# Linear attention and two MLP layers: the squared layer's scale moved into the norm's weights, its sign and offset into later steps, a padded last chunk, and all pair sums made on chip

## Chip, cores and metric

One core of a Trainium2 chip runs the whole program. The metric is device time in microseconds (us) of one execution; it was measured three times, and one more execution was profiled. Engines are named as in the profile: PE (TensorE) with PEld for its weight loads, DVE (VectorE), ACT (ScalarE), POOL (GpSimd), SP (SyncE, which issues the transfers). PSUM is the memory that PE writes, in banks of 128 x 512.

## The reference, cut to what matters

```
kv  = einsum('bhsd,bhse->bhde', k, v)          # 8 batches, 8 heads, 576 positions, 64 wide
o   = einsum('bhsd,bhde->bhse', q, kv)
x   = o / sqrt(mean(o*o, -1) + 1e-6) * g_norm  # then 4608 tokens x 512
h   = x @ w_in1;  r = maximum(h, 0)
x   = (s * (r*r) + b) @ w_out1                 # 2048 hidden columns; s and b are single numbers
h   = x @ w_in2
out = (h * sigmoid(h)) @ w_out2
```

## The kernel before

All is fp32. A wide product is made of three passes (`mm3`): each operand is split into a rounded part, made by ACT (`rnd`), and the rest, made by DVE or POOL (`rest`), and high x high, high x low and low x high are summed in one PSUM bank.

Tokens come in nine blocks of 512. Attention runs for a pair of heads of one batch at a time (`attention_pair`): `kv` sums k'v over four chunks of 128 positions and a last one of the remaining 64, for two heads that stand in two halves of the columns; `normalize` squares, sums, takes the root and multiplies by the weights `gn`. The first layer treats blocks 0 to 4 as they come (`unit`: one block and 128 hidden columns, 80 units). In a unit PE makes h in 12 passes, ACT applies three steps to it in its bank (`first`, `squares`, `affine`) and rounds it (`g_hi`), DVE makes the rest (`g_lo`), and PE takes 12 more passes into four accumulator banks.

Blocks 5 to 8 of the first layer, and blocks 0 to 3 and 5 to 8 of the second, are taken two at a time as six pairs (`tp` 0 to 5, of which 0 and 1 are of the first layer). A pair replaces each 2 x 2 block product by seven products of sums (Strassen-Winograd). Sums of inputs come from `pair_direct` (loads of the blocks, four sums each for two column parts, rounding by ACT, rest by POOL), except in the last two pairs: their sums are formed by POOL out of the results of pairs 0 and 1 (`results`, line 1153), stored in `xt_d`, and loaded by `pair_x`. `hidden` makes the seven products into three banks and forms the hidden values; for the first layer each gets relu, square and the affine step (L1023, L1026, L1029) before DVE forms the further sums (`add_up`, L1005). `outputs` sums seven results over four quarters: the first is copied out of its accumulator bank (`copy`, L223 or L225), the others are added by DVE (L1109). `results` combines them on POOL (L1134). The last block of the second layer runs as plain units at the end.

Meanwhile the weights are decoded, split and summed in quarters of 128 x 256 (`rq`; L405 sums, L216 rounding, L219 rests) and kept in DRAM for the pairs.

What order stands on each engine is decided when the program is built: `Plan` takes every step with an engine and a cost in us, a key, and what it needs and gives, and lists them by when they could begin. So a change of a cost or a step shifts the order on all engines. Costs are the plan's own, such as

```
add({"PE": 0.97}, key, kv, needs=..., makes=[f("kv")], takes=[b["psk"]], gives=...)
add({ACT: 0.68}, u + 0.25, affine, needs=[("sq", u)], makes=[("aff", u)])
```

Names in rows: `kv_ps`, `o_ps`, `r_ps`, `m_ps` are banks of the attention, `h` and `hp` hold hidden values of units and pairs, `acc` accumulators, `tmp` temporaries of a pair, `ya` a pair's results, `gh` and `g` split hidden values, `xo` split inputs, `vecs` single columns for norm weights, s and b.

## Time and profile before

| | |
|---|---|
| three runs, us | 1588.6, 1588.15, 1590.71; median 1588.6 |
| the profiled execution, us | 1589.08, its span 1587.3 |
| mean granted PE clock | 0.997 of 2.4 GHz |
| busy, us | PE 1558.8 (98%), DVE 1075.8 (68%), ACT 914.3 (58%), POOL 641.6 (40%) |
| transfers | 366.49 MB, mean 231 GB/s |

The span runs from the first to the last instruction; the execution's time holds some 1.8 us around it. Passes of PE overlap, so a record's length (0.39 us for a wide one) is more than the distance from one start to the next. A row of grouped instructions names line, engine, operation, output and inputs, shape and count, then busy time, the mean of one in ns, and the idle time before them with what ended it. Lines are those of the kernel before unless the change is spoken of.

### The profile page before, as it was taken

The page shows a single profiled execution, that of the slowest core. Times are in us where ns is not written, and L with a number is a line of the kernel's source. Part 1 is how long each engine was busy: PE and PEld are TensorE (multiplying, and loading weights), DVE is VectorE, ACT ScalarE, POOL GpSimd, SP SyncE. Part 2 cuts the span into 40 slices and gives each one's busy share as a digit, 9 for nine tenths or more (in the row PEclk, how much of TensorE's full clock was granted, in tenths as well). Part 3 has the DMA queues.
Part 4 walks back from the last instruction along what each step waited for, and adds up shares of the span by engine and source line. Part 5 has one row for each costly group of instructions (what it writes and reads, how often), then busy time and mean ns, then how long its engine had stood idle before and what let it go on. Part 6 is the DMA issues. An engine that isn't in the chain of part 4 may idle for free.

```text
span 1587.3 us, 23243 instructions
## 1 busy us (share of the span) xinstructions
PE 1558.8 (98%) x7393; PEld 1263.9 (80%) x7393; DVE 1075.8 (68%) x1937; ACT 914.3 (58%) x1779; POOL 641.6 (40%) x585
## 2 busy tenths in 40 slices
PE   8999999999999999999899999999999999999999
PEld 6777888778878878887787888888888888888887
DVE  5787678877666568888788856765666566656521
ACT  5897667667677677676667443544354444444222
POOL 1331122122124234478637862762277237622410
PEclk9999999999999999999999999999999999999999
DMA  9665688987557768888988896878687767776684
GB/s 212 186 190 137 227 256 274 277 242 234 186 173 235 260 208 277 266 272 280 294 267 281 289 310 189 255 200 238 197 281 193 237 200 242 188 240 196 205 201 141
DMA packets 354395, 366.49 MB, mean 231 GB/s; under 512 B 175712, under 2 KB 237152, under 8 KB 354272
## 3 DMA queue, kind: packets, MB, share of 16 engines
q1 hardware_dynamic: 354144, 365.00, 76.1%
q8 instruction: 59, 0.97, 0.3%
q14 instruction: 64, 0.52, 0.1%
q0 software_dynamic: 128, 0.00, 0.0%
HBM read 274.73 MB, written 90.18 MB: 230 GB/s over the span
## 4 chain that ended last, share of the span: by engine, by line
PE 49%; DVE 2%; ACT 1%; POOL 1%; DMA 1%; issue 1%; ACTq 0%; POOLq 0%; DVEq 0%
PE hp L966 21%; PE acc L1100 8%; PE acc L1102 7%; PE acc L1101 7%; PE acc L775 1%; PE acc L773 1%; PE acc L774 1%; PE h L211 1%; PE h L213 1%; PE h L212 1%; DVE rq L219 1%; DMA wo<-rq 0%; DMA x<-y 0%; ACT g L216 0%; POOL g L219 0%
## 5 line engine op out<-in xcount | busy, mean ns | idle before, releaser
L966 PE MATMUL hp<-xo,win 128*128 128x512 f32 x2016 | 512.8, 393 | 4.2 <-DVE g L219 3.1
L966 PEld LDWEIGHTS hp<-xo,win 128*128 128x128 f32 x2016 | 379.0, 189 | 90.7 <-DVE g L219 3.5
L219 POOL TENSOR_TENSOR g<-tmp,g 128x512 fp32r<-128x512 f32 x192 | 248.7, 1304 | 312.4 <-ACT g L216 272.3
L1109 DVE TENSOR_TENSOR ya<-acc,ya 128x512 f32<-128x512 f32 x252 | 172.9, 688 | 164.5 <-PE acc L1102 157.8
L1100 PE MATMUL acc<-g,wout 128*128 128x512 f32 x672 | 265.2, 395 | 6.5 <-DVE ya L225 5.0
L1101 PE MATMUL acc<-g,wout 128*128 128x512 f32 x672 | 264.1, 393 | 0.0
L1102 PE MATMUL acc<-g,wout 128*128 128x512 f32 x672 | 264.0, 393 | 0.0
L1100 PEld LDWEIGHTS acc<-g,wout 128*128 128x128 f32 x672 | 126.6, 188 | 35.3 <-DVE ya L225 5.9
L1102 PEld LDWEIGHTS acc<-g,wout 128*128 128x128 f32 x672 | 126.7, 189 | 28.6
L1101 PEld LDWEIGHTS acc<-g,wout 128*128 128x128 f32 x672 | 126.5, 188 | 27.3
L736 ACT ACTIVATE h<-h 128x512 f32<-128x512 f32 x96 | 56.0, 583 | 146.5 <-PE h L213 146.1
L216 ACT ACTIVATE g<-tmp 128x512 fp32r<-128x512 f32 x192 | 119.4, 630 | 27.8 <-DVE tmp L1005 14.8
L211 PE MATMUL acc<-gh,wo 128*128 128x512 f32 x320 | 132.0, 413 | 1.2 <-ACT gh L216 1.1
L1134 POOL TENSOR_TENSOR ya<-ya 128x512 f32<-128x512 f32 x84 | 109.0, 1324 | 46.4 <-DVE ya L1109 37.0
L211 PE MATMUL h<-xh,wi 128*128 128x512 f32 x320 | 127.3, 398 | 0.0
L212 PE MATMUL acc<-gh,wo 128*128 128x512 f32 x320 | 125.9, 393 | 1.4 <-DVE gh L219 1.4
L212 PE MATMUL h<-xl,wi 128*128 128x512 f32 x320 | 125.7, 393 | 0.4 <-DVE xl L219 0.4
L213 PE MATMUL h<-xh,wi 128*128 128x512 f32 x320 | 125.6, 393 | 0.0
L213 PE MATMUL acc<-gh,wo 128*128 128x512 f32 x320 | 125.5, 392 | 0.1
L325 POOL TENSOR_TENSOR rq<-raw 128x256 uint32<-128x256 uint32 x72 | 45.6, 633 | 184.0 <-DVE raw L311 109.2
L991 DVE TENSOR_TENSOR tmp<-hp,tmp 128x512 f32<-128x512 f32 x144 | 98.9, 687 | 31.0 <-PE hp L966 28.1
L219 DVE TENSOR_TENSOR g<-hp,g 128x512 fp32r<-128x512 f32 x144 | 98.6, 685 | 28.0 <-ACT g L216 25.7
(147 smaller groups left out, 2650.4 us busy)
## 6 DMA issues: line engine op xcount, KB each, us to landing
wout<-wo SPq DMA_DIRECT2D x368, 256.0 KB, 4.0
win<-wi SPq DMA_DIRECT2D x144, 512.0 KB, 5.0
wi<-rq SPq DMA_DIRECT2D x96, 256.0 KB, 2.9
wo<-rq SPq DMA_DIRECT2D x96, 256.0 KB, 3.3
win<-wi SPq DMA_DIRECT2D x80, 256.0 KB, 4.0
raw<-in_moe_w_out_dram SPq DMA_DIRECT2D x38, 256.0 KB, 4.5
raw<-in_moe_w_in_dram SPq DMA_DIRECT2D x34, 256.0 KB, 4.2
q<-in_q_dram SPq DMA_DIRECT2D x112, 72.0 KB, 2.7
```

The source lines that it names most:

```text
L211: nc.tensor.matmul(ps, wh, xh, start=first, stop=False)
L212: nc.tensor.matmul(ps, wh, xl, start=False, stop=False)
L213: nc.tensor.matmul(ps, wl, xh, start=False, stop=last)
L216: nc.scalar.activation(hi, src, AF.Copy)
L219: eng[e].tensor_tensor(lo, src, f32(hi), op=ALU.subtract)
L966: nc.tensor.matmul(to, w[:, wn, f_], x_[:, xn], start=first and n == 0, stop=kk == KH - 1 and n == 2, skip_group_check=True)
L991: nc.vector.tensor_tensor(t, bank[me, a], tmp[b_, me], op=ALU.add)
L1100: nc.tensor.matmul(to, w[:, 0, dd], gh, start=a == 0, stop=False)
L1101: nc.tensor.matmul(to, w[:, 0, dd], gl, start=False, stop=False)
L1102: nc.tensor.matmul(to, w[:, 1, dd], gh, start=False, stop=a == 1)
L1109: nc.vector.tensor_tensor(y2[tp, i, d], st["ps"], y2[tp, i, d], op=ALU.add)
L1134: eng[e].tensor_tensor(y2[tp, i, d], y2[tp, i, d], y2[tp, j, d], op=ALU.add)
```

## The change

1. The norm's weights are multiplied by the root of |s|, so that the square of relu already carries |s|. Ten small steps on DVE and a root on ACT at the program's start form that root (with one step of refinement), the sign of s (`sgn`) and b times the sign (`b1`, `b_neg`).
2. The affine step goes from units and from values of a pair that stand in banks. b enters where values are rounded (`rnd` and `rest` with a shift) and in three of the sums of a pair; for values in temporaries a step that adds b alone stays.
3. The sign is applied where accumulators of the first layer are copied or summed (`copy` with a factor, and the totals).
4. The last chunk of positions is padded with zeros to 128 rows (`rem_t`, set once at the start).
5. `pair_x`, `xt_d` and POOL's subtractions for it go; all six pairs use `pair_direct`.
6. The keys of block 4's attention stand closer (1.6 in place of 2.5), and plan costs follow: 0.73 for `kv`, 0.62 for a shifted rounding.

```
-    def rnd(hi, src):
-        nc.scalar.activation(hi, src, AF.Copy)
+    def rnd(hi, src, shift=None):
...
+            nc.scalar.activation(hi, src, AF.Identity, bias=shift)
-    def rest(e, lo, src, hi):
-        eng[e].tensor_tensor(lo, src, f32(hi), op=ALU.subtract)
+    def rest(e, lo, src, hi, shift=None):
...
+            eng[e].scalar_tensor_tensor(out=lo, in0=src, scalar=shift, in1=f32(hi), op0=ALU.add, op1=ALU.subtract)
+    def copy(e, dst, src, factor=None):
+        if factor is not None:
+            if e == "ACT":
+                nc.scalar.activation(dst, src, AF.Identity, scale=factor)
+            else:
+                eng[e].tensor_scalar(dst, src, factor, None, op0=ALU.mult)
...
-        add({"PE": 0.97}, key, kv, ...
+        add({"PE": 0.73}, key, kv, ...
...
         if layer == 0:
             add(act(T), u + 0.2, squares, needs=[src], makes=[("sq", u)])
-            add({ACT: 0.68}, u + 0.25, affine, needs=[("sq", u)], makes=[("aff", u)])
-            src = ("aff", u)
+            src = ("sq", u)
...
-            rnd(st["g"][0], h_t[u])
+            rnd(st["g"][0], h_t[u], b1 if layer == 0 else None)
...
-    def pair_x(tp, i, kk):
...
+                    nc.vector.scalar_tensor_tensor(out=t, in0=a(), scalar=shift, in1=b_(), op0=ALU.add, op1=op)
...
+                    nc.vector.scalar_tensor_tensor(out=y2[tp, i, d], in0=st["ps"], scalar=sgn, in1=y2[tp, i, d], op0=ALU.mult, op1=ALU.add)
...
-                    def go(e, dst=dst, a=a, b_=b_, d=d):
-                        eng[e].tensor_tensor(y2[tp, dst, d], y2[tp, a, d], y2[tp, b_, d], op=ALU.subtract)
...
+        rem_t = ap.tile([P, 2, 2 * D], F32, name="rem_t")
+        lent["rem"] = lend("wo12")
+        for t in (lent["rem"], rem_t):
+            nc.gpsimd.memset(t[REM:], 0.0)
...
+        nc.vector.tensor_scalar(sgn, s_t, 0.0, 2.0, op0=ALU.is_ge, op1=ALU.mult)
+        nc.vector.tensor_scalar(sgn, sgn, -1.0, None, op0=ALU.add)
+        nc.vector.tensor_tensor(mag_s, s_t, sgn, op=ALU.mult)
+        nc.scalar.activation(root, mag_s, AF.Sqrt)
+        nc.vector.tensor_scalar(guess, root, 1e-30, None, op0=ALU.max)
+        nc.vector.reciprocal(guess, guess)
+        nc.vector.scalar_tensor_tensor(out=root, in0=mag_s, scalar=guess, in1=root, op0=ALU.mult, op1=ALU.add)
+        nc.vector.tensor_scalar(root, root, 0.5, None, op0=ALU.mult)
+        nc.vector.tensor_tensor(gn, g0, root, op=ALU.mult)
+        nc.vector.tensor_tensor(b1, b_t, sgn, op=ALU.mult)
+        nc.vector.tensor_scalar(b_neg, b1, -1.0, None, op0=ALU.mult)
...
-            if made_by(pr) is None:
-                pair_direct(pr)
-            else:
-                for kk in range(KH):
-                    for i in range(7):
-                        pair_x(pr, i, kk)
+            pair_direct(pr)
```

The order on the engines moves almost everywhere. Counted over the program, ACT has 1695 instructions where it had 1781, DVE 1927 where it had 1939, POOL 589 where it had 590, and SP issues 20 transfers fewer; PE's passes are as many as before, but for one more warm-up pass. Three places follow.

DVE at the program's start, before, from the sums for `pairs_of` to the first differences of the attention:

```order
L1205 TENSOR_TENSOR pairs_of<-ident 128x2x32 x2
L514 STREAM_TRANSPOSE lent_wi_203<-lent_wo_153 128x576
L219 TENSOR_TENSOR kvl<-lent_wi_126,kvh 128x128
L225 COPY orem<-r_ps 128x64
L219 TENSOR_TENSOR qTl<-lent_wi_203,qTh 128x512
```

The same place after the change (`vecs` holds s, its root, its sign and the weights):

```order
L1167 TENSOR_TENSOR pairs_of<-ident 128x2x32 x2
L1175 TENSOR_SCALAR vecs<-vecs 128x1
L1176 TENSOR_SCALAR vecs<-vecs 128x1
L1177 TENSOR_TENSOR vecs<-vecs 128x1
L1179 TENSOR_SCALAR vecs<-vecs 128x1
L1180 RECIPROCAL vecs<-vecs 128x1
L1181 SCALAR_TENSOR_TENSOR vecs<-vecs 128x1
L1182 TENSOR_SCALAR vecs<-vecs 128x1
L1183 TENSOR_TENSOR vecs<-vecs 128x1
L1184 TENSOR_TENSOR vecs<-vecs 128x1
L1185 TENSOR_SCALAR vecs<-vecs 128x1
L517 STREAM_TRANSPOSE lent_wi_218<-lent_wo_166 128x576
```

Ten steps on single columns have come ahead of the first transpose.

DVE where pair 0 ends and pair 1 has begun, before (`rq` are weight quarters, `ya<-acc` is a copy that frees an accumulator bank):

```order
L991 TENSOR_TENSOR tmp<-hp,tmp 128x512 x2
L405 TENSOR_TENSOR rq<-rq 128x256
L219 TENSOR_TENSOR g_8387<-hp,g_8387 128x512
L405 TENSOR_TENSOR rq<-rq 128x256
L219 TENSOR_TENSOR rq<-rq 128x256 x5
L1005 TENSOR_TENSOR hp<-hp,tmp 128x512
L225 COPY ya<-acc 128x512
```

After the change:

```order
L958 TENSOR_TENSOR tmp<-hp,tmp 128x512 x2
L412 TENSOR_TENSOR rq<-rq 128x256
L220 TENSOR_TENSOR g_8265<-hp,g_8265 128x512
L229 TENSOR_SCALAR ya<-acc,vecs 128x512
L412 TENSOR_TENSOR rq<-rq 128x256
L220 TENSOR_TENSOR rq<-rq 128x256 x4
L229 TENSOR_SCALAR ya<-acc,vecs 128x512
```

The run of differences is four long instead of five, and one copy out of an accumulator stands ahead of it.

POOL at the same place, before (L1134 sums results of pair 0, L1153 makes sums for the second layer):

```order
L1134 TENSOR_TENSOR ya<-ya 128x512 x2
L219 TENSOR_TENSOR g_8351<-tmp,g_8351 128x512
L1134 TENSOR_TENSOR ya<-ya 128x512 x7
L1153 TENSOR_TENSOR ya<-ya 128x512 x7
L219 TENSOR_TENSOR g_8422<-tmp,g_8422 128x512
L1153 TENSOR_TENSOR ya<-ya 128x512
```

After the change:

```order
L220 TENSOR_TENSOR rq<-rq 128x256
L220 TENSOR_TENSOR g_8227<-tmp,g_8227 128x512
L332 TENSOR_TENSOR rq<-raw 128x256
L1110 TENSOR_TENSOR ya<-ya 128x512 x6
L412 TENSOR_TENSOR rq<-rq 128x256
L1110 TENSOR_TENSOR ya<-ya 128x512
L220 TENSOR_TENSOR rq<-rq 128x256 x3
L1110 TENSOR_TENSOR ya<-ya 128x512
```

POOL's eight subtractions are gone, and four differences of quarters have come to it.

## Rows read from the trace of the kernel before

**Rows 1.** The page, first part: busy time, share of the span, instructions.
```profile
PE 1558.8 (98%) x7393; PEld 1263.9 (80%) x7393; DVE 1075.8 (68%) x1937; ACT 914.3 (58%) x1779; POOL 641.6 (40%) x585
```

**Rows 2.** Busy time by stretch: length, engines (instructions), granted clock, DMA share, GB/s.
```profile
0.00:50.00 50.00, 43.02 (x369) 32.92 (x370) 32.00 (x64) 29.50 (x66) 10.69 (x19) 1.00 0.92 208
50.00:125.00 75.00, 73.38 (x369) 58.43 (x369) 61.69 (x108) 67.72 (x129) 25.40 (x23) 1.00 0.63 172
125.00:150.00 25.00, 21.35 (x119) 16.27 (x119) 18.73 (x44) 18.58 (x47) 3.73 (x6) 0.93 0.79 193
150.00:550.00 400.00, 398.18 (x2102) 321.54 (x2101) 284.95 (x639) 272.40 (x595) 90.86 (x111) 1.00 0.75 232
550.00:700.00 150.00, 146.88 (x636) 120.31 (x635) 116.21 (x202) 109.60 (x211) 70.56 (x69) 0.99 0.80 258
700.00:856.00 156.00, 149.96 (x645) 121.61 (x644) 125.93 (x218) 106.69 (x201) 99.94 (x88) 0.99 0.86 283
856.00:1012.00 156.00, 154.40 (x671) 125.46 (x670) 110.22 (x170) 77.33 (x141) 98.71 (x81) 1.00 0.78 254
1012.00:1475.00 463.00, 463.00 (x2019) 378.47 (x2018) 294.44 (x452) 208.31 (x357) 221.43 (x175) 1.00 0.75 222
```

**Rows 3.** Instructions of PE grouped by line and shape: the 64-row products.
```profile
L500 PE MATMUL kv_ps<-rem 64*64 64x64 f32 x112 | 9.4, 246 | 0.0
```

**Rows 4.** Timeline of PE near 197 us: start, length, what, count.
```profile
196.95 0.40 PE L213 MATMUL h<-xh,wi 128*128 128x512 f32 x1
197.28 0.69 PE L500 MATMUL kv_ps<-kv 128*64 128x64 f32 x16
197.89 0.33 PE L500 MATMUL kv_ps<-rem 64*64 64x64 f32 x4
198.16 0.50 PE L211 MATMUL acc<-gh,wo 128*128 128x512 f32 x1
```

**Rows 5.** Instructions of ACT grouped by line and shape, in units.
```profile
L742 ACT ACTIVATE h<-h,vecs 128x512 f32<-128x512 f32 x80 | 59.7, 747 | 1.1
...
L216 ACT ACTIVATE gh<-h 128x512 fp32r<-128x512 f32 x80 | 47.7, 596 | 0.8
L739 ACT ACTIVATE h<-h 128x512 f32<-128x512 f32 x80 | 46.9, 586 | 1.2
```

**Rows 6.** Instructions of DVE grouped by line and shape.
```profile
L219 DVE TENSOR_TENSOR rq<-rq 128x256 fp32r<-128x256 f32 x155 | 77.9, 540 | 7.7 <-ACT rq L216 6.5
L219 DVE TENSOR_TENSOR gh<-h,gh 128x512 fp32r<-128x512 f32 x80 | 54.8, 685 | 44.2 <-ACT gh L216 43.5
...
L609 DVE SCALAR_TENSOR_TENSOR x<-o_ps,vecs,sq 128x512 f32<-128x512 f32 x20 | 14.9, 743 | 0.3
...
L909 DVE TENSOR_TENSOR x<-x,xr 128x512 f32<-128x512 f32 x7 | 6.8, 973 | 0.0
```

**Rows 7.** Timelines of POOL, DVE and PE at the end of pair 0.
```profile
745.43 9.86 POOL L1134 TENSOR_TENSOR ya<-ya 128x512 f32<-128x512 f32 x7
748.37 7.20 DVE L219 TENSOR_TENSOR rq<-rq 128x256 fp32r<-128x256 f32 x5
756.82 0.50 PE L1100 MATMUL acc<-g,wout 128*128 128x512 f32 x1 [3.62 <-DVE ya L225]
```

**Rows 8.** The start: timelines of DVE and POOL, the scalar's landing, a memory set.
```profile
9.30 0.78 DVE L514 STREAM_TRANSPOSE lent_wi<-lent_wo 128x576 f32<-128x576 f32 x1 [7.59 <-DMA lent_wo<-in_q_dram]
10.00 0.25 DVE L219 TENSOR_TENSOR kvl<-lent_wi,kvh 128x128 fp32r<-128x128 f32 x1
13.29 0.78 DVE L514 STREAM_TRANSPOSE lent_wi<-lent_wo 128x576 f32<-128x576 f32 x1 [1.80 <-DMA lent_wo<-in_q_dram]
3.73 0.57 POOL L1211 DMA_DIRECT2D vecs<-in_moe_s_dram  x1
DMA to landing us min/median/max: 3.8/3.8/3.8
L1198 POOL MEMSET lent_wi<- 128x512 f32 x1 | 0.5, 524 | 0.0
```

More of the change, by code (lines that the diff above doesn't have):

```diff
@@ L184, in layer_of @@
         return 0 if tp < NL1 else 1
-    def made_by(tp):
-        return tp - NPR if tp >= NPR else None
     NTMP = 7
@@ L545, in attention_pair @@
         prev, prev_r = ([], []) if z else ([("x32",) + before], [("ro",) + before])
-        add({"PE": 0.97}, key, kv, needs=[f("k"), f("v"), ("kr",) + fr, ("vr",) + fr] + prev_r, makes=[f("kv")],
+        add({"PE": 0.73}, key, kv, needs=[f("k"), f("v"), ("kr",) + fr, ("vr",) + fr] + prev_r, makes=[f("kv")],
             takes=[b["psk"]], gives=[b["kv"], ("wo12", 0) if z else b["rem"]])
@@ L739, in squares @@
             nc.scalar.activation(h_t[u], h_t[u], AF.Square)
-        def affine(e):
-            nc.scalar.activation(h_t[u], h_t[u], AF.Identity, scale=s_t, bias=b_t)
         add(act(T), u + 0.1, first, needs=[("mm1", u, KD - 1)], makes=[("r", u)])
@@ L753, in g_hi @@
             st["g"] = place2(gs)
-            rnd(st["g"][0], h_t[u])
+            rnd(st["g"][0], h_t[u], b1 if layer == 0 else None)
         def g_lo(e):
-            rest(e, st["g"][1], h_t[u], st["g"][0])
-        add(act(T), u + 0.3, g_hi, needs=[src], makes=[("gh", u)], takes=[gs])
+            rest(e, st["g"][1], h_t[u], st["g"][0], b1 if layer == 0 else None)
+        add({ACT: 0.62} if layer == 0 else act(T), u + 0.3, g_hi, needs=[src], makes=[("gh", u)], takes=[gs])
         add({DVE: 0.69}, u + 0.35, g_lo, needs=[("gh", u)], makes=[("gl", u)], gives=[("h", u)])
@@ L812, in out_y @@
                 st["y"] = ring(yb)
-            copy(e, st["y"], a_t[d])
+            copy(e, st["y"], a_t[d], None if final else sgn)
         def store(e):
@@ L1026, in square, with raised @@
                 nc.scalar.activation(src_of(src), src_of(src), AF.Square)
-            def affine(e, src=src):
-                nc.scalar.activation(src_of(src), src_of(src), AF.Identity, scale=s_t, bias=b_t)
+            def raised(e, src=src):
+                nc.scalar.activation(src_of(src), src_of(src), AF.Identity, bias=b1)
             sf = ("sg", src) + me
@@ L1049, in hidden, with hi, lo @@
             gb = ("g2", me + (i,))
-            def hi(e, src=src, i=i, gb=gb):
+            shift = b1 if i == B21 and not layer_of(tp) else None
+            def hi(e, src=src, i=i, gb=gb, shift=shift):
                 g2[me, i] = place2(gb)
-                rnd(g2[me, i][0], src_of(src))
-            def lo(e, src=src, i=i):
-                rest(e, g2[me, i][1], src_of(src), g2[me, i][0])
-            add(act(T), kk, hi, needs=ready, makes=[("gh",) + me + (i,)], takes=[gb])
+                rnd(g2[me, i][0], src_of(src), shift)
+            def lo(e, src=src, i=i, shift=shift):
+                rest(e, g2[me, i][1], src_of(src), g2[me, i][0], shift)
+            add(act(T) if shift is None else {ACT: 0.62}, kk, hi, needs=ready, makes=[("gh",) + me + (i,)], takes=[gb])
             add({DVE: 0.69} if src in in_bank else {POOL: Port(1.3)}, kk + 0.03, lo, needs=[("gh",) + me + (i,)],
@@ L1137, in results @@
             if not layer_of(tp):
[L1138 to L1158 removed]
+                for c, n, i, ready in parts:
+                    add({"SP": 0.48}, key + 0.3, lambda e, n=n, c=c, i=i, d=d: dma(y1[BLOCKS[tp][n]][:, c * KH + d], y2[tp, i, d]),
+                        needs=[o(ready)], makes=[("y", BLOCKS[tp][n], c * KH + d)], gives=[y(i)], move=0.73)
                 continue
@@ L1188 @@
         nc.vector.memset(zeros, 0.0)
-        vecs = const.tile([P, 4], F32, name="vecs")
+        vecs = const.tile([P, 11], F32, name="vecs")
         curve0 = const.tile([P, 1], F32, name="curve0")
-        eps, gn, s_t, b_t = (vecs[:, i:i + 1] for i in range(4))
+        eps, gn, s_t, b_t, sgn, mag_s, root, guess, b1, b_neg, g0 = (vecs[:, i:i + 1] for i in range(11))
         nc.vector.memset(eps, 1e-6)
```

88 lines of the change are left out of this document (26 added, 62 removed).

## The prediction

> **What bounds the kernel now.** I read the page's first lines, then the table of stretches, then single places. TensorE (PE) is busy for 1558.8 of the 1587.3 us [rows 1]: whatever shortens the kernel must take work out of PE's queue or remove a wait in it. The stretches [rows 2] say where PE waits. From 1012 us on there is no idle time at all (463.00 of 463.00). In the first 50 us it is 7.0 us, much of the rest there is warm-up work on zeros, and the DMA engines are at 0.92: that start is bound by the transfers. Between lie the waits that can be won. From 50 to 550 us (first layer, plain blocks) they are 1.62, 3.65 and 1.82 us, 7.1 in all; from 125 to 150 us the granted clock is 0.93, which is 0.07 x 25 = 1.75 us of work more; together 8.8 us. From 550 to 1012 us (the two first-layer pairs and the start of the third) they are 3.12, 6.04 and 1.60 us, 10.8 in all, and two stretches at a clock of 0.99 add 0.01 x 306 = 3.1; together 13.8 us. ScalarE (ACT) is at 67.72 of 75 us in the second stretch, VectorE (DVE) at 125.93 of 156 us in the sixth: both close behind PE.
>
> The profiled execution took 1589.1 us (1587.3 and 1.8 around it), 0.5 above the median of 1588.6. I make the sum against 1589.1 and take 0.5 off at the end.
>
> **The padded chunk.** This is the term that shortens PE's own queue. Of each of the 28 key-value products behind the start, the last chunk is 64 rows high: 112 records, 4 for each [rows 3]. In one place [rows 4] the last wide product before it starts at 196.95 and the first of 16 records of 128x64 at 197.28: 0.33, where wide ones follow each other at 0.23 (2019 in 463.00 us [rows 2]), so 0.10 for the change of form. The 16 take 0.61 us up to the 64-row ones, those 0.27 to the next wide product: 0.88 in all, with two changes of form (to 64 rows, back to full). After the change all 20 records have one form. The 16 without a change of form are (0.61 - 0.10) / 16 = 0.032 each, so 20 are 0.64; with the way back at 0.10 it is 0.74, a gain of 0.14; were the way back free, 0.24. No row shows the way back from 128x64 directly. I take the middle, 0.19: 28 x 0.19 = 5.3 us off, bounds 3.9 and 6.7. The four products at the start lie among warm-up work and count nothing. The added memory sets on GpSimd (POOL) are two at the start.
>
> **The affine step in first-layer units.** ACT loses 80 instructions of 747 ns, and the rounding behind, now with a bias from memory, grows. A square is 586 ns and the affine step with two operands from memory 747, 80 for each: the rounding goes from 596 to some 676 [rows 5]. Per unit ACT does 0.67 us less, and a result is ready 0.67 us sooner. On DVE the 80 differences become three-operand instructions: 743 against 685 ns, 58 ns more each [rows 6]. PE takes 24 wide products for a unit, over 5 us, so DVE's 0.06 is hidden as long as PE leads; ACT's relief shows only where PE waits for it. From 50 to 550 us the 8.8 us above are such waits or their clock, in a stretch with ACT at 90%. I take half, 4.4 off. Bounds: 8.8 (all), and nothing.
>
> **The pairs.** In the first-layer pairs ACT loses 32 affine steps on banks, of the form that takes 747 ns in the units [rows 5]; the 32 on temporaries stay, with one operand fewer. DVE has 48 sums or differences, 16 bank differences and 84 totals in the longer form: 148 x 58 ns = 8.6 us over two pairs, 4.3 each, on an engine that was at 126 of 156. The copies with the sign cost ACT 80 ns more (26) and leave DVE fewer. The 16 subtractions of sums on POOL go, and with them 16 stores and 16 loads of a separate tensor; in return the last two pairs make their sums on the spot, eight each. DVE gets 15 more of these, at up to 0.97 us [rows 6], in a stretch with DVE at 294 of 463 us and PE without a wait. This costs nothing while DVE keeps a third of its time free; without this cover the first products of a pair would wait for one sum, about 1 us twice. SP loses 20 transfers.
>
> The dearest single wait stands where POOL's result sums and DVE meet [rows 7]. POOL runs seven sums end to end from 745.43 for 9.86 us. DVE's five differences of weight quarters take 7.20 us there, 1.44 each, against a mean of 540 ns [rows 6]. Behind them in DVE's queue stands the copy of an accumulator, and PE, which needs that bank, resumes at 756.82 after waiting 3.62 us for it. In that stretch PE loses 6.04 us of idle time and 1.56 of clock, 7.6. In the new order the eight subtractions behind POOL's sums are gone and POOL takes four of the differences itself; DVE's run is four, with one accumulator copy now ahead of it. The wait shrinks rather than vanishes; DVE's dearer forms work against it. Of the 13.8 us of these stretches I take two fifths, 5.5 off. Bounds: 13.8 off, and more waiting than before (first rival).
>
> **The start.** DVE now carries ten tiny steps ahead of the first transpose, and ACT a root ahead of its first copy; both wait for the scalar, whose transfer POOL issues at 3.73 and which lands 3.8 later. Two memory sets come ahead of the issue: 512 columns take 524 ns, so 1024 and 256 some 1.3 us: the landing comes at about 8.8. Ten steps and ACT's hop I put at 0.2 to 0.25 each, by the 0.25 of a small difference [rows 8]; so the first transpose, which stood at 9.30, comes 1.7 to 2.2 late. But DVE idles 1.80 us until 13.29 for the next transfer [rows 8]. The delay is absorbed but for 0.2 or so, which I take as 0; if the transfers did not pace the start, 2 us would be lost.
>
> **Sum.** 5.3 + 4.4 + 5.5 = 15.2 off: 1589.1 - 15.2 = 1573.9, less 0.5: **1573.4 us**. Its own range is 1565 to 1582: two thirds of the 22.6 us of waits with 6.7 for the padding give 1566.8, a fifth of them with 3.9 gives 1580.2.
>
> **Rivals.** *Slower: the collision at the pairs' ends multiplies.* A run of four or more quarter differences on DVE, inside a run of POOL sums, with an accumulator copy behind: from about four on the wait exceeds what PE's open banks cover. The new DVE order still has such runs, and its dearer forms leave less slack. Four such places at 7.6 us in place of the 13.8 are 30.4 - 13.8 = 16.6 more; with the padding's 5.3 off the result is 1588.6 + 11.3 = 1599.9. Against it: POOL's run is shorter, and before only one place of this kind cost so much. The Trainium skill, "GPSIMD Engine Reference", section Specifications, says that POOL's way to SBUF is shared with VectorE and contended by VectorE instructions with two SBUF inputs. The 1.44 against 0.54 us bear it out; by that rule the 15 sums that move to DVE would be stretched as well and would stretch POOL's. Chance 0.08.
>
> *Only the padding shows.* The waits are of the order, not of ACT's load; a new order has as many. Then 1588.6 - 5.3 = 1583.3. For it: PE's waits end at several engines, and at the dear one ACT was not the late one. Chance 0.16.
>
> *The padding does nothing.* If 64-row records owed their 0.27 us only to the way back, which stays, full-height ones would be no cheaper. Then the waits alone count: 1588.6 - 9.9 = 1578.7. The Trainium skill, "TensorEngine Tiling (Array Packing)", section Theoretical Speedup, states a gain of up to 2x from tiles where a dimension is 64 or less; by it the padding gives a gain away. The trace doesn't bear it out: 0.27 for four against 0.032 each is the other way. Chance 0.08.
>
> *Nothing in sum.* New waits, at the start too, eat the 5.3: 1588. Chance 0.06.
>
> **How the numbers follow.** The forecast has 0.62. It, the second and the third rival are faster by over 0.2% (3.2 us, about what a measurement tells from no change): 0.86, less 0.01 for the upper edge of the second. Within 0.2%: 0.07. Slower: 0.08. The range runs from 1565 to 1586, over the second and third rival; what lies outside is the fourth, the slower case, and the far ends of the waits.
>
> **What would show it.** The last-chunk records join the others at one form, and a key-value product takes about 0.7 us where it took 0.88; four ACT instructions per first-layer unit become three, the last of some 680 ns; DVE's totals in the first pairs take some 745 ns. PE's idle time falls by half from 50 to 550 us, and by less from 550 to 1012; from 1012 to the end there is none, with sums on DVE in all pairs. DVE's second transpose still waits for its transfer. It would be wrong if the idle time from 550 to 1012 us grew, or if PE waited for a sum at the head of the last two pairs.

## The result, and the profile after

The changed kernel takes **1562.3 us** (median of four runs, 1561.59 to 1563.72) where the kernel before took 1589.26 in the same session: a ratio of 0.9833, 95% interval 0.982 to 0.9846, 27 us off. The forecast was 1573.4 with a range of 1565 to 1586: the direction was right, the size was missed, and the time lies 2.7 us below the range.

Page of the changed kernel, first part, to be read against [rows 1]:

```profile
PE 1539.7 (99%) x7394; PEld 1259.0 (81%) x7394; DVE 1084.5 (69%) x1925; ACT 854.7 (55%) x1693; POOL 635.1 (41%) x584
```

Busy time by stretch of the changed kernel, to be read against [rows 2], same columns:

```profile
0.00:50.00 50.00, 45.02 (x382) 35.15 (x383) 35.00 (x75) 30.51 (x70) 11.88 (x21) 0.97 0.89 220
50.00:125.00 75.00, 72.38 (x362) 56.51 (x361) 60.56 (x106) 60.45 (x116) 26.52 (x23) 1.00 0.62 165
125.00:150.00 25.00, 18.50 (x108) 14.63 (x107) 15.41 (x36) 14.46 (x38) 3.85 (x6) 0.86 0.75 186
150.00:550.00 400.00, 399.66 (x2132) 325.44 (x2131) 295.12 (x638) 245.43 (x556) 88.98 (x109) 1.00 0.77 236
550.00:700.00 150.00, 149.07 (x658) 122.93 (x657) 119.98 (x203) 103.70 (x202) 81.55 (x78) 1.00 0.84 267
700.00:856.00 156.00, 156.00 (x690) 129.17 (x689) 131.51 (x213) 104.86 (x201) 104.51 (x94) 1.00 0.87 289
856.00:1012.00 156.00, 154.96 (x680) 126.85 (x679) 109.68 (x173) 73.12 (x132) 86.72 (x74) 1.00 0.78 249
1012.00:1475.00 463.00, 463.00 (x2039) 381.51 (x2038) 300.72 (x462) 204.51 (x351) 218.41 (x171) 1.00 0.74 215
```

Four things are to be seen. From 700 to 856 us PE's 6.04 us of idle time are gone, and half clock with them. From 125 to 150 us PE is worse off: 18.50 us busy where it was 21.35, the clock at 0.86 where it was 0.93. In the last row nothing waited before and nothing waits now, and yet PE passes 2039 wide products in 463 us instead of 2019. And PE's own busy time fell by 19.1 us (1558.8 to 1539.7), of which the padding's 4.1 (below) are a small part.

I added up the distances between the starts of PE's records in both profiles (spans 1587.3 and 1560.5, 26.8 apart). "Small excess" is what wide products that follow each other take beyond 226.7 ns, up to 250; "waits" are longer distances (over 350 ns between wide products, over 380 around the attention's), with the half clock behind the longest ones: from 580.4 to 583 us of the kernel before, behind a wait of 3.1 us, the granted clock is 0.50 (1.2 GHz) and wide products stand 427 ns apart.

| part of PE's time, us | before | after | change | in the prediction |
|---|---|---|---|---|
| small excess, whole span | 13.8 | 2.8 | -11.1 | 0 |
| 28 key-value products | 0.88 each | 0.73 each | -4.1 | -5.3 |
| waits, 50 to 550 us | 11.3 | 13.1 | +1.8 | -4.4 |
| waits, 550 to 1012 us | 15.0 | 2.6 | -12.4 | -5.5 |
| the rest, start included | | | -1.0 | 0 |

The two terms for waits missed in opposite ways and make 10.6 together, where 9.9 was foretold: that this comes near is luck. What is missing in the sum is the first line; the others make 15.7, beside the 15.2 of the prediction.

The durations came out as priced. PE near 199 us in the changed kernel (start, length, what, count), against [rows 4]:

```profile
198.82 0.40 PE L210 MATMUL acc<-gh,wo 128*128 128x512 f32 x1
199.15 0.69 PE L503 MATMUL kv_ps<-kv 128*64 128x64 f32 x16
199.67 0.29 PE L503 MATMUL kv_ps<-rem_t 128*64 128x64 f32 x4
199.88 0.50 PE L208 MATMUL o_ps<-qTh,kvh 128*128 128x512 f32 x1
```

From the first record to the next wide product it is 0.73 us where it was 0.88. Record by record it is 1.393 us from the start of the wide product ahead to the start of the second one behind, against 1.538: 0.145 each, and 28 x 0.145 = 4.1, near my lower bound of 3.9. The way back from 128x64 to wide records costs its 0.10 after all.

Groups of the changed kernel by line and shape (against [rows 5, 6]):

```profile
L1085 DVE SCALAR_TENSOR_TENSOR ya<-acc,vecs,ya 128x512 f32<-128x512 f32 x84 | 62.4, 748 | 26.4 <-PE acc L1076 25.5
L222 DVE SCALAR_TENSOR_TENSOR gh<-h,vecs,gh 128x512 fp32r<-128x512 f32 x80 | 59.3, 742 | 36.8 <-ACT gh L216 36.6
L216 ACT ACTIVATE gh<-h,vecs 128x512 fp32r<-128x512 f32 x80 | 54.6, 683 | 1.0
```

The rounding with a bias takes 683 ns (676 foretold), the differences 742 and the totals 748 (743 foretold).

At the start (DVE's timeline of the changed kernel, against [rows 8]):

```profile
8.44 0.15 DVE L1175 TENSOR_SCALAR vecs<-vecs 128x1 f32<-128x1 f32 x1 [6.73 <-DMA vecs<-in_moe_s_dram]
10.51 0.78 DVE L517 STREAM_TRANSPOSE lent_wi<-lent_wo 128x576 f32<-128x576 f32 x1
13.17 0.78 DVE L517 STREAM_TRANSPOSE lent_wi<-lent_wo 128x576 f32<-128x576 f32 x1 [0.39 <-DMA lent_wo<-in_q_dram]
```

The scalar lands near 8.4, the ten steps take 2.1, the first transpose comes 1.2 us late, and the second waits for its transfer as before: the delay is absorbed, as the prediction had it.

### The profile page after: what moved, and what is told of

It reads as the page before. It is cut to its first block, busy times and chain, and to the rows that moved or that the text cites. A ratio compares the mean times of both kernels' runs of the same rounds, so it can differ in the third digit from the quotient of the medians.

```text
span 1560.5 us, 23102 instructions
## 1 busy us (share of the span) xinstructions
PE 1539.7 (99%) x7394; PEld 1259.0 (81%) x7394; DVE 1084.5 (69%) x1925; ACT 854.7 (55%) x1693; POOL 635.1 (41%) x584
## 4 chain that ended last, share of the span: by engine, by line
PE 89%; DMA 4%; SPq 2%; DVE 2%; ACT 1%; issue 1%; POOL 0%; DVEq 0%; ACTq 0%
PE hp L933 28%; PE acc L1074 9%; PE acc L1075 9%; PE acc L1076 9%; PE h L208 5%; PE h L209 5%; PE h L210 5%; PE acc L208 4%; PE acc L209 4%; PE acc L210 4%; SPq L236 2%; DMA raw<-in_moe_w_out_dram 1%; PE kv_ps L503 1%; PE acc L773 1%; PE acc L772 1%; PE acc L774 1%
## 5 line engine op out<-in xcount | busy, mean ns | idle before, releaser
L1074 PE MATMUL acc<-g,wout 128*128 128x512 f32 x672 | 261.8, 390 | 0.8 <-DVE ya L1085 0.5
L1076 PE MATMUL acc<-g,wout 128*128 128x512 f32 x672 | 261.6, 389 | 0.0
L1075 PE MATMUL acc<-g,wout 128*128 128x512 f32 x672 | 261.5, 389 | 0.0
L1083 DVE TENSOR_TENSOR ya<-acc,ya 128x512 f32<-128x512 f32 x168 | 115.7, 689 | 128.3 <-PE acc L1076 120.6
L214 ACT ACTIVATE g<-tmp 128x512 fp32r<-128x512 f32 x192 | 119.3, 629 | 24.4 <-PE acc L1076 10.3
L993 ACT ACTIVATE hp<-hp 128x512 f32<-128x512 f32 x96 | 55.6, 582 | 95.6 <-DVE hp L973 95.3
```

What stands on the lines that cost most here:

```text
L214: nc.scalar.activation(hi, src, AF.Copy)
L1074: nc.tensor.matmul(to, w[:, 0, dd], gh, start=a == 0, stop=False)
L1075: nc.tensor.matmul(to, w[:, 0, dd], gl, start=False, stop=False)
L1076: nc.tensor.matmul(to, w[:, 1, dd], gh, start=False, stop=a == 1)
L1083: nc.vector.tensor_tensor(y2[tp, i, d], st["ps"], y2[tp, i, d], op=ALU.add)
```

## Experiments

### Where do 11 us of small excess come from?

A wide product reads a moving operand of 512 columns and weights of 128 columns, both from SBUF, the memory in which tiles lie. Where they stand within a partition's row is fixed when the program is built. The constants' tile `vecs` grew from 4 to 11 columns, 32 bytes after rounding, and with it every tile that is allocated from the lower end moved up by 32 bytes; tiles from the upper end (the late weights, `rq` and five of the pairs' `g` buffers) stayed. Wide products by the places of their operands modulo 256 bytes:

```
moving, weights      before      after
agree                5442        6432
differ by 32 bytes    990           0
```

In the second-layer pairs of the kernel before, every product whose moving operand lay in one of those five buffers had an interval of mostly 230 to 237 ns, and the five or so behind it were still late; with the others it was 227. 11.1 us over 990 products are 11 ns each. The change was not meant to do this. Three kernels move tiles alone, with each engine's order word for word as in the kernel they come from:

```
before_shift32, of the kernel before:
-        vecs = const.tile([P, 4], F32, name="vecs")
+        vecs = const.tile([P, 9], F32, name="vecs")
after_shift32, of the changed kernel:
-        vecs = const.tile([P, 11], F32, name="vecs")
+        vecs = const.tile([P, 17], F32, name="vecs")
after_shift64, of the changed kernel:
-        vecs = const.tile([P, 11], F32, name="vecs")
+        vecs = const.tile([P, 25], F32, name="vecs")
```

> The kernel before with a constants' tile of nine columns instead of four: every left-hand tile moves up by 32 bytes, the order on all engines stays word for word. Theory A (moving operand and weights at different offsets within 64 bytes make a wide product slower): wide products of the second-layer pairs fall from 229.5 to about 227 ns from start to start, and the whole from 1589.3 to about 1578 (13.8 us of small excess over 226.7 ns, less the 2.8 that the changed kernel keeps, is 11.1). Theory B (the spacing comes from the order of the work, or from the tiles that lie high in memory): no change, 1587 to 1591.

> The changed kernel with its constants' tile of 17 columns instead of 11: 32 bytes further, so the two ends of memory differ again within 64 bytes; order unchanged. Theory A: wide products in the second-layer pairs go back to 229 to 230 ns, and 1562.3 becomes about 1572 to 1574. Theory B: 1561 to 1564.

> The changed kernel with 25 columns, 64 bytes further: both ends agree within 64 bytes as in the changed kernel. Theory A: no change, 1561 to 1564, wide products at 227 ns. A third theory (any move of tiles matters, by their distance to others or by the bank they fall into): another time, by several us.

The stretch from 1012 to 1475 us, busy time by engine as above, of before_shift32:

```profile
1012.00:1475.00 463.00, 463.00 (x2039) 381.57 (x2038) 297.25 (x457) 208.30 (x357) 216.17 (x171) 1.00 0.76 223
```

of after_shift32:

```profile
1012.00:1475.00 463.00, 463.00 (x2025) 379.05 (x2024) 300.45 (x462) 204.15 (x350) 216.19 (x169) 1.00 0.73 215
```

and of after_shift64:

```profile
1012.00:1475.00 463.00, 463.00 (x2022) 378.29 (x2021) 302.94 (x464) 205.59 (x352) 214.61 (x168) 1.00 0.74 215
```

| kernel | median, us | ratio to before, interval | small excess, us |
|---|---|---|---|
| before_shift32 | 1580.1 (1575.99 to 1585.38) | 0.9948 (0.993 to 0.9966) | 2.4 |
| changed kernel | 1562.3 | 0.9833 (0.982 to 0.9846) | 2.8 |
| after_shift32 | 1566.83 | 0.9859 (0.9844 to 0.9875) | 11.0 |
| after_shift64 (two runs) | 1572.28 | 0.9894 (0.9873 to 0.9914) | 11.8 |

32 bytes in the constants bring the kernel before to the changed kernel's 2039 products and take 9.3 us off by the medians, 8 by the ratio (5 to 11 by its interval, as its runs scatter); 32 or 64 bytes more in the changed kernel bring the excess back. The 64 bytes were meant as the control for which nothing should change, and theory A fell there: agreement within 64 bytes is not enough. In after_shift64 lower and upper tiles differ by 64 of 256 bytes, in after_shift32 by 32, in 1020 products each. Of the 8.2 us of excess that after_shift32 gained, 6.1 show between the two profiles and 4.5 between the medians; where the rest went I did not settle.

The first run of products alone, align_alone, seemed to speak against the whole idea:

```
    both0 = ps.tile([P, T], F32, name="both0")
    for _ in range(3 * N):
        nc.tensor.matmul(both0, w(0), m(0), start=True, stop=True)
...
    for _ in range(3 * N):
        nc.tensor.matmul(mov8, w(0), m(8), start=True, stop=True)
```

> Wide products on zeros and nothing else (attention and both layers are left out), 240 for each case: both operands at offset 0 within 64 bytes (line 39), both at 32 (43), only the moving one at 32 (47), only the weights at 32 (51), and three that take turns (57, 61, 65). Theory A with moving operand against weights: 227 ns each on lines 39 and 43, 231 to 236 on lines 47 and 51. Where the weights loaded at the same time for the next product decide, line 61 (each product's own two agree, the next weights differ) is slow and line 65 (own differ, next agree) fast; where its own weights decide, the other way round. Theory B: 227 everywhere.

All lines came out at 230 to 234 ns, lines 39 and 43 too (232.4 and 233.3). But its two tiles began at addresses 128 bytes apart modulo 256, so no case agreed in the sense that after_shift64 had left open. align_apart sets the distance:

```
    def go(i, n, o, w):
        nc.tensor.matmul(bank[i % 2], sta[:, w:w + P], mov[:, o:o + T], start=(i < 2), stop=(i >= n - 2))
...
    for i in range(2 * N):
        go(i, 2 * N, 16, 0)
```

> Wide products on zeros alone again (attention and both layers are left out), both tiles now beginning at the same place within 256 bytes, 160 products for each distance of the moving operand from the weights: 0 (line 32), 32 (35), 64 (38), 128 (41), 192 (44), 256 (47) and 512 bytes (50); then both moved by 32 (53), taking turns with each own pair agreeing (56), and with each product agreeing with the next product's weights instead (59). Theory C (a wide product takes 227 ns where the moving operand and the weights read beside it stand at the same place within 256 bytes, else 230 to 236): 227 on lines 32, 47, 50 and 53, 230 to 236 on 35, 38, 41 and 44; the place decides by own weights if line 56 is fast and 59 slow, by the next ones if the other way round. Rival (products alone always run at 232, as in the first run of this kind, and the place does not matter): 230 or more on every line.

All its records carry the one line of `go`, so the cases are told apart by time. Stretches of 30 us, one in each case in the order of the expectation (PE's products in 30 us are the first count):

```profile
24.50:54.50 30.00, 30.00 (x134) 24.82 (x134) 0.00 (x0) 0.00 (x0) 0.00 (x0) 1.00 0.00 1
61.50:91.50 30.00, 30.00 (x130) 24.10 (x129) 0.00 (x0) 0.00 (x0) 0.00 (x0) 1.00 0.00 1
98.50:128.50 30.00, 30.00 (x133) 24.62 (x132) 0.00 (x0) 0.00 (x0) 0.00 (x0) 1.00 0.00 1
135.50:165.50 30.00, 30.00 (x131) 24.32 (x130) 0.00 (x0) 0.00 (x0) 0.00 (x0) 1.00 0.00 1
172.50:202.50 30.00, 30.00 (x130) 24.16 (x129) 0.00 (x0) 0.00 (x0) 0.00 (x0) 1.00 0.00 1
209.50:239.50 30.00, 30.00 (x134) 24.82 (x133) 0.00 (x0) 0.00 (x0) 0.00 (x0) 1.00 0.00 1
246.50:276.50 30.00, 30.00 (x134) 24.86 (x133) 0.00 (x0) 0.00 (x0) 0.00 (x0) 1.00 0.00 1
282.50:312.50 30.00, 30.00 (x134) 24.80 (x134) 0.00 (x0) 0.00 (x0) 0.00 (x0) 1.00 0.00 1
319.50:349.50 30.00, 30.00 (x130) 24.07 (x130) 0.00 (x0) 0.00 (x0) 0.00 (x0) 1.00 0.00 1
357.50:387.50 30.00, 30.00 (x132) 24.48 (x132) 0.00 (x0) 0.00 (x0) 0.00 (x0) 1.00 0.00 1
```

From start to start that is 226.7 ns at a distance of 0, 256 and 512 bytes and with both moved by 32; 233.3 at 32, 228.9 at 64, 232.4 at 128 and 233.3 at 192. Nothing else runs, so neither order nor another engine can be the cause: theory C holds, but for the 228.9 at 64, less than its 230. Whether a product's own weights or the next ones decide is not settled: with own agreement it is 233.3, with agreement with the next 230.0, and neither is free. Nor does the size carry over: 64 bytes cost 2.2 ns a product here, but as much excess as 32 bytes in the kernel (11.8 against 11.0 us). What else adds to it there stays open.

### Which part took the pairs' waits away?

In all kernels from here on but before_pad, every wide product has its operands at one place within 256 bytes (ring_only, no_fold and before_cost carry the nine columns of before_shift32 for it). "Fold" is the scale in the norm's weights with all that follows from it, "ring" the sums on the spot.

```
ring_only, of the kernel before (pair_x, xt_d and POOL's subtractions gone):
-            if made_by(pr) is None:
-                pair_direct(pr)
...
+            pair_direct(pr)
fold_only, of the kernel before (with the ten steps, the sign and the shifts):
-            add({ACT: 0.68}, u + 0.25, affine, needs=[("sq", u)], makes=[("aff", u)])
-            src = ("aff", u)
+            src = ("sq", u)
no_ring: the changed kernel without ring_only's edit
no_fold: the changed kernel without fold_only's edit
```

> The kernel before with the scale in the norm's weights, sign and offset in the later steps and the ten steps at the start, but the last chunk unpadded, the pairs' sums by POOL as before and the old keys; its larger constants' tile brings all tiles to one place within 256 bytes, so it stands beside before_shift32 (1580.1). Theory (each dear wait has its own cause): the 3.5 us near 573 and the four waits of 0.5 to 0.9 near 447, 469 and 503 us go (together some 4.5 with the half clock behind the first), the 4.2 near 747 us stays, 1574 to 1577; and a new wait of over 3 us near 135 us comes, as in the two runs with the fold so far, which would give 3 of it back. Rival (order alone): waits fall anywhere, those near 447 to 503 among them.

> The kernel before with all pairs' sums made on the spot and nothing else; tiles at one place within 256 bytes, so it too stands beside before_shift32 (1580.1). Theory: the 4.2 us near 747 falls under 1.5, the 3.5 near 573 and the small ones near 447 to 503 stay, no wait of over 3 us near 135; 1573 to 1577. Rival: the dear wait stays because DVE's own five differences make it.

> The changed kernel with the sums of the last two pairs made as before (by POOL out of results, stored and loaded); tiles at the same place within 256 bytes as in the changed kernel. Theory R (the waits between 550 and 1012 us went because POOL lost those subtractions): waits of PE and half clock there go from 2.6 back to about 10 us or more, 1570 to 1575. Theory F (they went with the affine step and its ACT time) or O (with the order alone): 1560 to 1565 and 1555 to 1575 without a pattern.

> The changed kernel with the affine step kept in units and pairs (weights of the norm, rounding, sums and copies as before, no steps for the root at the start); padded chunk, sums on the spot and keys as in the change. Theory F: waits between 550 and 1012 us come back, about 10 us, and those between 150 and 550 us grow from 0.8 to some 3; 1572 to 1576. Theory R: within 2 us of the changed kernel, 1560 to 1565.

| kernel | median, us | ratio to before, interval | waits 50 to 550, us | waits 550 to 1012, us |
|---|---|---|---|---|
| before_shift32 (neither) | 1580.1 | 0.9948 (0.993 to 0.9966) | 11.9 | 13.9 |
| fold_only | 1571.35 | 0.9887 (0.9864 to 0.9911) | 8.9 | 12.1 |
| ring_only | 1575.22 | 0.991 (0.9888 to 0.9931) | 13.7 | 10.3 |
| no_ring (fold, padding, keys) | 1573.74 | 0.9899 (0.9883 to 0.9916) | 14.3 | 10.3 |
| no_fold (ring, padding, keys) | 1569.53 | 0.9874 (0.9849 to 0.9899) | 12.0 | 11.5 |
| changed kernel (all) | 1562.3 | 0.9833 (0.982 to 0.9846) | 13.1 | 2.6 |

The waits are read from one profile of each kernel. Each dear wait has its own cause. PE's waits from 550 to 1012 us by whom it waited for (total, times, longest, in us), in ring_only:

```profile
PE hp L930 <- DVE g L216: 3.1, 1, 3.1
PE hp L930 <- DVE tmp L955: 2.9, 3, 1.9
```

in fold_only:

```profile
PE acc L1114 <- DVE ya L232: 2.9, 1, 2.9
PE acc L1114 <- ACT ya L230: 2.6, 1, 2.6
```

and in the changed kernel, its two longest:

```profile
PE hp L933 <- DVE g L220: 0.9, 1, 0.9
PE acc L1074 <- DVE ya L1085: 0.5, 1, 0.5
```

Without the fold the wait of 3.1 us for a difference of hidden values stays, and ACT is the late one (ACT's and PE's timelines of ring_only):

```profile
575.47 0.81 ACT L993 ACTIVATE tmp<-tmp,vecs 128x512 f32<-128x512 f32 x1
576.34 1.15 ACT L213 ACTIVATE g<-tmp 128x512 fp32r<-128x512 f32 x2
577.39 0.80 ACT L993 ACTIVATE tmp<-tmp,vecs 128x512 f32<-128x512 f32 x1
578.10 0.57 ACT L213 ACTIVATE g<-hp 128x512 fp32r<-128x512 f32 x1
579.45 0.73 PE L930 MATMUL hp<-xo,win 128*128 128x512 f32 x2 [3.12 <-DVE g L216]
```

ACT works from 572.3 to 580.2 all but without a break, affine steps (L993) among it, and the rounding that DVE's difference needs (578.10) comes last. With the fold that place costs 0.4 to 1.4 us from start to start in every run. Without the ring change it is the result buffers (ACT's timeline of no_ring, then POOL's, then PE's):

```profile
748.32 8.98 POOL L1165 TENSOR_TENSOR ya<-ya 128x512 f32<-128x512 f32 x7
761.78 0.69 ACT L230 ACTIVATE ya<-acc,vecs 128x512 f32<-128x512 f32 x1 [1.40 <-DMA xt_d<-ya]
762.52 0.50 PE L1110 MATMUL acc<-g,wout 128*128 128x512 f32 x1 [3.68 <-ACT ya L230]
```

In no_ring POOL's subtractions and the stores to `xt_d` hold the tiles `ya`; the copy that frees an accumulator bank needs one, and PE needs the bank. In the kernel before, the copy of [rows 7] follows DVE's run of differences without a pause, so its trace shows no wait for a `ya` tile there. And ring_only keeps the run of five differences beside POOL's sums (DVE, then PE):

```profile
745.88 7.25 DVE L216 TENSOR_TENSOR rq<-rq 128x256 fp32r<-128x256 f32 x5
753.79 0.50 PE L1064 MATMUL acc<-g,wout 128*128 128x512 f32 x1 [0.46 <-DVE ya L222]
```

The run lasts as long as in [rows 7], and the wait is 0.46 where it was 3.62. What differs is that ACT has by then copied four accumulators (736.2, 740.1, 741.5 and 746.0 us) where it had copied three (738.6, 743.9 and 748.4), so PE passes 12 more products, 2.7 us, before it needs the bank. That the missing subtractions leave a `ya` tile for this copy fits no_ring; for the kernel before it is not shown. With one of the two edits another wait takes the place of the one removed (12.1 and 10.3 are left of 13.9); with both, 2.6 are left (4.1 in a second profile of the same kernel, after_again below). The sum of the single gains, 1.8 and 3.6, is less than half of 11.3. Beside their expectations, ring_only came out as its theory had it and no_ring as theory R; no_fold got its waits back as theory F had it, but took 2.5 us less than its range; fold_only took 2.7 us less than its theory, and the wait near 135 us that was to give 3 us back did not come.

The small waits near 447 to 503 us, 0.5 to 0.9 each for DVE's difference in a unit, stand in before_shift32, ring_only and no_fold and in neither fold_only nor no_ring: in these orders they belong to the affine step, as foretold. The fold does not keep the place clear in every order: no_pad, old_cost and orem2_cost (below), all with the fold, lose 2.2 to 2.4 us from start to start near 467 to 469 us for the same difference. old_key gives the last piece, the spacing of block 4's attention:

```
-        seq = [(t, p, KF * (t - 1) + (0.5 + (3.2 if t < LB else 1.6) * p if t > 1 else 0.75 + 3.4 * p)) for t in range(1, TP) for p in range(NP)]
+        seq = [(t, p, KF * (t - 1) + (0.5 + (3.2 if t < LB else 2.5) * p if t > 1 else 0.75 + 3.4 * p)) for t in range(1, TP) for p in range(NP)]
```

> The changed kernel with the key spacing of the fifth block's attention at 2.5 as before, all else as changed. Theory: those keys touch nothing ahead of 300 us, so the wait of 4.8 near 135 us stays; the small waits near 447 to 503 us stay away, as the affine step is gone: 1561 to 1565. Rival (the keys, not the fold, took them away): they are back, and the time is some 3 us longer.

It took 1564.08 (0.9834, 0.9818 to 0.9851): no difference from the changed kernel, and those waits stayed away.

### What is the padding worth, and what is the new wait near 135 us?

```
before_pad, of the kernel before (rem_t and its zeros as in the change, cost 0.97 kept):
-            t2 = lent["rem"][:, :, 2 * p * D:2 * (p + 1) * D] if z else st["rem"]
+            t2 = lent["rem"][:, :, 2 * p * D:2 * (p + 1) * D] if z else rem_t
no_pad: the changed kernel without the padding, cost 0.97
old_cost, of the changed kernel (before_cost is the reverse in the kernel before):
-        add({"PE": 0.73}, key, kv, ...
+        add({"PE": 0.97}, key, kv, ...
```

> The kernel before with the padded last chunk alone; the plan's cost of that step stays at 0.97, so that the order stays, and tiles stay at their places. My theory of the padding: a key-value product takes 0.73 where it took 0.88, 28 x 0.145 = 4.1 us off, 1585.3. Rival (the gain came with the order, or is given back in the next wait): 1588 to 1590.

> The changed kernel with the last chunk of 64 rows as before and its old plan cost; fold, sums on the spot, keys and places in memory as changed. If the padding is worth its 28 x 0.145 = 4.1 us: 1566 to 1567. If the padding brings the wait of 4.8 us near 135 us with its half clock (gone here), both cancel: 1560 to 1563, PE further on at 150 us (some 425 wide products instead of 402), key-value products at 0.88.

> The changed kernel, padded, with the plan's old cost of 0.97 for the key-value product in place of 0.73: the work is the same, only the order moves. If the order makes the wait near 135 us: it goes, 1557 to 1560. If the shorter product makes it (PE comes sooner to a bank that is still held): it stays, 1561 to 1565.

> The kernel before with the new plan cost of 0.73 alone, the work unchanged (64 rows), tiles at one place within 256 bytes: beside before_shift32 (1580.1) it shows what another order alone is worth. If waits have causes in the work: the 3.5 us near 573 and the 4.2 near 747 stay, 1577 to 1583. If the order makes them: one of them falls or grows by over 2 us.

| kernel | median, us | ratio to before, interval | waits 50 to 550, us | waits 550 to 1012, us |
|---|---|---|---|---|
| before_pad | 1588.41 | 0.9988 (0.9978 to 0.9999) | 12.3 | 15.5 |
| before_cost | 1578.85 | 0.9935 (0.9919 to 0.9951) | 15.5 | 13.5 |
| no_pad | 1569.25 | 0.9875 (0.9855 to 0.9894) | 12.1 | 2.6 |
| old_cost | 1566.5 | 0.9865 (0.9844 to 0.9887) | 14.6 | 3.5 |

In the kernel before the shorter product is worth 1.6 to 1.9 of its 4.1 us. The time is the rival's (1588 to 1590) and not the theory's (1585.3): waits around the attention grow (11.3 to 12.3 us up to 550) because PE only comes sooner to what it waits for. In the changed kernel the padding with its cost is worth 4.7 to 7 us by the medians (against after_again, below, and against its first four runs), more than the 4.1 that the records show and the 1566 to 1567 foretold for no_pad: in no_pad another order brings a wait of 2.4 near 467 us. before_cost, where nothing but the order moved, grows a wait of 4.7 at the same place while the two dear waits of the pairs stay, 1.2 us from before_shift32 in the whole. So the pairs' waits outlast this new order, and those from 50 to 550 us are largely of the order, a few us either way with each new list. That answers the second rival's reason: it held for the units, not, in this test, for the pairs.

The new wait near 135 us (SP's, ACT's and PE's timelines of the changed kernel):

```profile
136.19 1.08 SPq L236 DMA_DIRECT2D orem_d<-orem  x1
140.02 0.21 ACT L231 COPY orem<-r_ps 128x64 f32<-128x64 f32 x1 [1.82 <-issue]
140.29 0.61 PE L593 MATMUL m_ps<-part,pairs_of 128*128 128x16 f32 x2 [4.42 <-DMA raw<-in_moe_w_out_dram]
```

The profile puts PE's 4.42 us down to raw weights. But PE goes on right after ACT's copy, which empties the bank `r_ps` into `orem`; there is one `orem`, and its store stood in SP's queue from the copy at 130.6 to 136.2, behind ten loads. A wait of over 2 us at this place stands in every kernel that has the fold and the new cost of 0.73 with one `orem` in the plan, and in no other: in no_pad and old_cost, with the fold and the old cost, the longest from 125 to 145 us are 1.1 and 0.8. So this order of the list makes it, and in no_ring and old_key the profile itself names ACT's copy into `orem`. old_cost won nothing by that (1566.5, where 1557 to 1560 was foretold), as its waits from 150 to 550 us grew by 5 to 6. orem2 gives a second buffer and tells the plan; orem_two gives the buffer alone, so that the order stays word for word; orem2_cost puts the old cost beside orem2's edit.

```
orem2 and orem_two, of the changed kernel:
-            st["orem"] = ap.tile([P, REM], F32, tag="orem", name="orem")
+            st["orem"] = ap.tile([P, REM], F32, tag="orem", name="orem", bufs=2)
orem2 alone:
-    plan = Plan({... "q": 1, "part": 2, ...
+    plan = Plan({... "q": 1, "orem": 2, "part": 2, ...
```

> The changed kernel with two buffers instead of one for the remainder of the attention's output, and a second place for it in the plan. Theory on the wait of 4.8 us near 135 us (the bank that PE waits for is freed by a copy into that buffer, which waits for the store before it in SP's queue): the wait goes, with the half clock behind it some 4 to 6 us, 1557 to 1560. Rival (the loads of attention and raw weights bound that stretch): PE waits as long a few us later, 1561 to 1564.

> The changed kernel with the second buffer for the remainder and the old plan cost together. If the start's waits are of the order and of that buffer: 1555 to 1560, the fastest of all; if what is won there is waited for later in the pairs, as with the buffer alone: 1561 to 1565.

> The changed kernel with two buffers for the remainder of the attention's output, and the plan not told: the order on all engines and the places in memory within 256 bytes stay. ACT's copy at 140.0 us then waits for nothing but its place in the queue, behind a rounding that ends at 138.2: the wait of 4.8 falls to about 3.0, PE is 1.8 us earlier, 1560.5 against 1562.3. Rival (the raw weights that ACT waits for ahead of it decide, or the pairs take it back): no difference, 1562 to 1563.

> The changed kernel itself, on the same chip as orem_two: 1561.5 to 1563.8, as in its four runs; wide products at 227 ns and PE's waits between 550 and 1012 us at 2 to 3 us. A different time, or other waits, would say that what the single profiles show is not the same in each run.

orem2 took 1563.33 (0.9838, 0.9818 to 0.9858), outside its theory's 1557 to 1560: the wait was gone, waits from 50 to 550 us fell from 13.1 to 9.4, and those of the pairs rose from 2.6 to 5.6, so nothing was won. orem2_cost took 1566.47 (0.9858, 0.984 to 0.9876), slower than both of its ranges. orem_two took 1560.87 (0.9824, 0.9809 to 0.984) beside 1564.58 for after_again (0.9842, 0.9826 to 0.9859). PE's longest wait from 125 to 145 us in orem_two:

```profile
PE m_ps L593 <- ACT orem L231: 3.2, 1, 3.2
```

and in after_again:

```profile
PE m_ps L593 <- DMA raw<-in_moe_w_out_dram: 4.8, 1, 4.8
```

With the second buffer the profile names the copy itself, and 1.6 us of the wait go, near the 1.8 expected. The 3.2 that are left come in the main from raw weights, which ACT waits for ahead of the copy in its queue (ACT's timeline of orem_two):

```profile
136.31 0.43 ACT L309 ACTIVATE rq<-raw 128x256 f32<-128x256 f32 x1 [2.98 <-DMA raw<-in_moe_w_in_dram]
137.27 0.19 ACT L231 COPY orem<-r_ps 128x64 f32<-128x64 f32 x1
```

The time agrees in direction, but the two intervals overlap: that orem_two beats the changed kernel is likely, not shown. after_again, with a median 0.8 us above its forecast, also shows how far one kernel's profile carries: the same waits stand at the same places, with 4.1 us instead of 2.6 in the pairs.

## Why the prediction was wrong, by its own steps

**The step that failed** is the one that took the distance of wide products as given, and so put what the change does to it at nothing; it measured 11.1 us. "This is the term that shortens PE's own queue", I wrote of the padding, and used 0.23 us between wide products from "2019 in 463.00 us" [rows 2] as a price. That row held the hint: 463.00 / 2019 is 229.3 ns, while the median distance of wide products in the same trace from 150 to 550 us is 227, and nothing in the rows gives a reason why a stretch in which PE never waits should be 1% slower. I read the diff's `vecs` with 11 columns as ten tiny steps, not as 32 bytes under every tile. before_shift32 shows that this alone is worth some 8 to 9 us of the 27; after_shift32 and after_shift64, the same change without that accident, take 1566.8 and 1572.3, inside the stated range.

**The padded chunk:** right in mechanism, 4.1 on PE against 5.3; the way back costs what the lower bound said. The third rival, that full height is no cheaper, is refuted by 1.393 against 1.538 us.

**Units, 50 to 550 us:** half of the term's reason was right. From 150 to 550 us the waits fell from 3.2 to 0.8, and fold_only and old_key show that the ones near 447 to 503 us went with the affine step. But I priced the stretch as one, and up to 150 us PE waits for something else: there they grew from 8.1 to 12.3, of which the wait at 135 is the largest. PE's idle time from 50 to 550 us, which was to fall by half, rose from 7.1 to 9.5 us. The "stretch with ACT at 90%" was misread as well: that is 50 to 125 us alone; from 150 to 550 us ACT was busy for 272.40 of 400 us [rows 2]. "I take half" stood on a stretch that mixed two causes.

**Pairs, 550 to 1012 us:** the places and causes were right, ACT's affine steps in one and the collision of POOL's sums with DVE and the accumulator copy in the other. "The wait shrinks rather than vanishes" was wrong: two fifths were taken, five sixths went. I had priced the length of DVE's run alone. Without the subtractions one more copy out of an accumulator comes ahead of the run, and no_ring shows that the subtractions and stores can also hold the `ya` tile that a copy needs. The slower rival did not come. The run of four differences still collides with POOL's sums, at 1.18 us each (DVE's timeline of the changed kernel):

```profile
737.32 4.72 DVE L220 TENSOR_TENSOR rq<-rq 128x256 fp32r<-128x256 f32 x4
```

But the copies behind it come in time, and PE has no idle time from 700 to 856 us.

**Start and last pairs:** both right at zero. From 1012 us on PE waits for nothing, with eight sums on the spot at the head of each of the last two pairs.

**The second rival** (only the padding shows, 1583.3) and the fourth fell with these.

## What to carry to other kernels

Before pricing what a change does to a bound engine, compare its steady distance from start to start with the best one in any run: here one per cent without a wait had a cause, the place of the operands. After any edit that adds or resizes a tile, list where moving operands and weights now stand modulo 256 bytes; here 32 bytes in a constants' tile were worth some 8 of 27 us. And where two engines are each late at neighbouring places, price the fixes together: here either alone left over 10 of 14 us, both left 2.6 and 4.1 in two profiles.

## What the runs showed of the hardware that I had not expected

In align_apart a wide fp32 product on TensorE follows the one ahead at 226.7 ns where its moving operand and its weights start at the same place modulo 256 bytes within a partition's row (distances of 0, 256 and 512), and at 228.9 to 233.3 where they differ by 32, 64, 128 or 192, at a granted clock of 1.00 and with no other engine at work. The Trainium skill, "SBUF — State Buffer", section Who interferes with whom, gives TensorE two independent read ports, one for the moving operand and one for the weights, and says that it never waits on anyone; by that rule every case of align_apart would stand at 226.7. The measurement differs, so the two reads are not free of each other. How they meet was not tried.

In the kernels, products that agree but follow one that doesn't were still 1 to 9 ns late for about five products, so that 990 differing products of 6432 cost some 11 us.
